# A recurrent segment loop with streamed weights: a step's small loads merged and laid out anew, and the output projection begun before the last group's values

## The chip, the cores and the metric

The kernel runs on one core of a Trainium2 chip. The metric is the device time of one execution in microseconds; the kernel before is given as the median of three runs.

## The reference, cut to what matters

Two independent parts share one launch. Part A is a long convolution over 2048 positions and 1024 channels; its result fills the first 1024 columns of the output. Part B is a recurrence over segments, and its result fills the other 1024:

```
kv = shift4(k, shift_k) * v
outA = q * (fftconv(kv, ssm_k) + kv * ssm_D)

mem = mem0                                  # 8 rows of 1024
for s in range(64):                         # segments of 32 rows of x
    h = concat([mem, x[32*s : 32*s+32]])    # 40 rows
    q, k, v = h @ Wq, h @ Wk, h @ Wv        # 32 heads of 128
    p = softmax(mask(q @ k^T / sqrt(128)))  # row i sees column j if i < 8 or j <= i
    o = (p @ v) @ Wo                        # 40 x 1024
    mem = o[:8]
    outB[32*s : 32*s+32] = o[8:]
```

Everything is bf16 at the borders. A step needs the eight output rows of the step before it, so the 64 steps can't overlap much; each reads all of Wq, Wk, Wv and Wo (8 MB each).

## The kernel before

The whole program is emitted in a manual schedule: each engine executes its instructions in the order in which the code issues them, and so does each DMA queue (SP's, ACT's and POOL's). Tiles of one tag share buffers, so a new tile waits until everything that reads or writes the old one has ended, its stores included.

**Prologue.** Part A is computed in stages by matmuls with Fourier matrices; its work runs up to about 0.3 ms. Interleaved with it, the class `Rows` (L126 to L193) does the work of Part B that doesn't depend on the recurrence: the projections of each segment's last eight rows of x (called memory-slot rows in the code), for all 64 segments at once. They are computed in twelve units, (q, g), (k, g) or (v, g), where g is one of four groups of eight heads. `half` runs half a block of matmuls, `evac` (L147) takes a block out of PSUM on ACT or DVE. When a k unit ends, the tile stq, which holds q and k of that group, is stored to QKBd in DRAM (L184, POOL's queue, 2 MB in runs of 16 KB); when a v unit ends, stv is stored to VBd (L187, POOL's queue, one DMA of 1 MB).

**Weights.** A pair is two weight blocks of [128, 1024] (512 KB). Most of the 64 pairs stay in SBUF, two are parked in PSUM and copied out by `unpark` (L715), and 17 are streamed in each step: STREAM (L40) lists which. `pairs` (L55) sets the order in which they are streamed. The ring has five buffers; `done` (L723) is called after a pair's last use, and `place` (L707) then issues the next pair's load on SP's queue, into the buffer that came free. So the loads stand in the order of use, and their order must be that of the steps.

**A step** (L906 to L967). hT holds the 32 rows of h: 8 of memory (from the step before) and 24 of x. For each group g: `qk_part` (L741) projects q and k with four column tiles of PE side by side into one PSUM bank, `qk_out` (L753) copies them to qks, `v_part` (L757) projects v into vacc and `v_out` (L770) copies it to vsb. `tr_a` (L780) transposes qks and writes QT and KT on DVE; KT also gets eight columns from qkb, the precomputed rows. `scores` (L801) makes S with the mask, `softmax` (L823) makes P and its transpose PT, `pv` (L836) multiplies by vsb and by VB (the precomputed values) in four PSUM tiles otacc, each evicted by ACT into OT; `wo` (L858) adds the group's contribution to Y. Within the loop, group g runs its own projections, scores and softmax of group g-1, and pv of group g-2. What is left for the tail (L943 on): wo of all groups, scores and softmax of group 3, pv of groups 2 and 3. At the end ACT copies Y to Y_sb, `fill_mem` (L885) transposes its first eight rows into the next hT, and the other 24 rows are stored by four DMAs on POOL's queue.

Small loads of a step:
- qkb, one per group, by `load_b` (L789) on SP's queue, issued in the group before: [128, 128] out of QKBd[g], 256 B per partition, 32 KB; two buffers.
- VB, by `load_vb` (L796), four DMAs of 16 KB on POOL's queue, issued in the tail ahead of group 3's wo.
- H, the 32 rows of x for the next step, by `load_h` (L652), one DMA of 64 KB on ACT's queue, issued at the start of group 2. It is read as "dq t c", a block of 32 rows for each quarter of the columns. H has the tag "st", as has Y_sb (L960): one buffer for both.
- OLd, a store of 64 KB on POOL's queue at the end of pv of group 3 (L856): it saves the attention output of the eight precomputed rows. Their output projection is done after the loop for all segments (L969 to L987).

Of the kernel before, what the change touches and what calls it, by code (L numbers as in the profile page):

```python
# [21 lines left out]
def fused_kernel(ctx: ExitStack, tc, q, k, v, shift_k, ssm_k, ssm_D, outa, x, mem0, Wq, Wk, Wv, Wo, outb, n_seg):  # L22
# [103 lines left out]
    class Rows:  # L126
# [27 lines left out]
        def half(self, n, by="A"):  # L154

            for _ in range(n):
# [21 lines left out]
                if lo:  # L178
                    if m == "v":
                        self.evac(self.sv[:, rb, cs], self.ps[:], by)  # L180
                    else:
                        self.evac(self.st[:, :, j, int(m == "k"), :], self.ps[:].rearrange("e (s r) -> e s r", r=8), by)
                    if m == "k" and j == 7:
                        nc.gpsimd.dma_start(QKBd[g].rearrange("e s x -> e (s x)"),  # L184
                                            self.st[:].rearrange("e s h t r -> e (s h t r)"))
                    if m == "v" and j == 7:
                        nc.gpsimd.dma_start(VBd.rearrange("(rb p) n -> p rb n", p=128)[:, :, g * 1024:(g + 1) * 1024],  # L187
                                            self.sv[:])
# [463 lines left out]
    def load_h(s):  # L652

        H_ = act.tile([128, 256], BF, tag="st", name="H")
        xq = x.rearrange("t (dq c) -> dq t c", dq=4)
        if s == 0:
            for dq in range(4):
                nc.gpsimd.dma_start(H_[32 * dq:32 * dq + 8, :], mem0[:, dq * 256:(dq + 1) * 256])
                nc.gpsimd.dma_start(H_[32 * dq + 8:32 * dq + 32, :], xq[dq, 0:24, :])
        else:  # L660
            nc.scalar.dma_start(H_[:], xq[:, 32 * s - 8:32 * s + 24, :])
        return H_

# [93 lines left out]
    def v_part(u, kcs):  # L757
        if kcs[0] == 0:
            u.vacc = ps_acc.tile([128, 512], F32, tag="acc", name="vacc")
        for kc in kcs:  # L760
            if kc % 2 == 0:
                w = pair(("v", u.g, kc // 2))
            for c in range(4):
                nc.tensor.matmul(u.vacc[32 * c:32 * c + 32, 0:256], lhsT=hT[:, kc, :],  # L764
                                 rhs=w[kc % 2][:, c * 256:(c + 1) * 256],
                                 start=(kc == 0), stop=(kc == 7), tile_position=(0, 32 * c))
            if kc % 2 == 1:
                done(("v", u.g, kc // 2))
# [11 lines left out]
    def tr_a(u):  # L780
# [4 lines left out]
        nc.vector.tensor_copy(u.KT[:, :, 32:40], u.qkb[:].rearrange("e (h t r) -> e t h r", h=8, t=2)[:, 1])  # L785
# [3 lines left out]
    def load_b(s, g):  # L789
        u = G()  # L790
        u.g = g
        u.qkb = act2.tile([128, 128], BF, tag="qkb", name="qkb")
        nc.sync.dma_start(u.qkb[:], QKBd[g][:, s, :])
        return u

    def load_vb(s):  # L796
        for c in range(4):
            nc.gpsimd.dma_start(VB[32 * c:32 * c + 32, :],  # L798
                                VBd[8 * s:8 * s + 8].rearrange("r (g c x) -> c g r x", g=4, c=4)[c])

    def scores(u):  # L801
        S = ps_ts.tile([128, 4, 40], F32, tag="ts", name="S")
        qb = u.qkb[:].rearrange("e (h t r) -> e h t r", h=8, t=2)
# [32 lines left out]
    def pv(u, s, cs, ts_bank=False):  # L836
# [3 lines left out]
        for c in cs:  # L840
            pool, tag = (ps_ts, "ts") if ts_bank and c == 2 else (ps_acc, "acc")
# [16 lines left out]
    def wo(u, Y, hhs=range(8)):  # L858
        for hh in hhs:
            if hh % 2 == 0:  # L860
                w = pair(("o", u.g, hh // 2))
            for dq in range(4):
                nc.tensor.matmul(Y[32 * dq:32 * dq + 32, 0:256], lhsT=u.OT[:, hh, 0:32],  # L863
                                 rhs=w[hh % 2][:, dq * 256:(dq + 1) * 256],
                                 start=(u.g == 0 and hh == 0), stop=(u.g == 3 and hh == 7),
                                 tile_position=(0, 32 * dq))
# [8 lines left out]
    def h_rows(H_, hT_, r0):  # L875
# [3 lines left out]
        for half in range(2):  # L879
# [3 lines left out]
            tp[:, 0:256].rearrange("p (hf dq r) -> p dq hf r", hf=2, dq=4)[:, :, :, r0:32])  # L883
# [15 lines left out]
    nxt = load_b(0, 0)  # L899
# [6 lines left out]
    for s in range(n_seg):  # L906
        us = []
        for g in range(4):
            if g == 2 and s + 1 < n_seg:
                H = load_h(s + 1)  # L910
# [5 lines left out]
            u = nxt  # L916
# [3 lines left out]
            if g < 3:  # L920
                nxt = load_b(s, g + 1)
            elif s + 1 < n_seg:
                nxt = load_b(s + 1, 0)
# [11 lines left out]
            v_part(u, range(0, 8))  # L935
            tr_a(u)
            v_out(u)
# [23 lines left out]
        nc.scalar.copy(Y_sb[:], Y[:, 0:256])  # L961
# [94 lines left out]
```

## Time and profile before

| | us |
|---|---|
| median of three runs | 2215.84 |
| lowest and highest run | 2213.84, 2217.09 |
| profiled execution, span on the core | 2198.5 |
| PE busy | 1808.6 (82%) |
| DVE busy | 1082.4 (49%) |
| ACT busy | 836.0 (38%) |
| POOL busy | 500.4 (23%) |

The profile's page gives the profiled execution's span, from its first instruction to its last, and no other time of that execution; the runs' times are taken from outside and are 17.3 us longer at the median. 732.29 MB moved by DMA in the span, 333 GB/s in the mean. How to read it: the share of an engine is over the whole span, which holds three different things, the prologue with Part A, the 64 steps, and the projection of the precomputed rows at the end; a window view cuts them apart. In the waits, "A <- B" means that A stood idle and B's end released it; the three numbers are the total in us, the number of times and the longest. In a timeline row stand the start, the duration, engine, line and operation, the output and the inputs, and in brackets the idle time before it with its releaser. The row of a DMA issue gives the time that the issuing queue took, not the transfer's.

### The profile page before, as it was taken

The page shows a single profiled execution, that of the slowest core. Times are in us where ns is not written, and L with a number is a line of the kernel's source. Part 1 is how long each engine was busy: PE and PEld are TensorE (multiplying, and loading weights), DVE is VectorE, ACT ScalarE, POOL GpSimd, SP SyncE. Part 2 cuts the span into 40 slices and gives each one's busy share as a digit, 9 for nine tenths or more (in the row PEclk, how much of TensorE's full clock was granted, in tenths as well). Part 3 has the DMA queues.
Part 4 walks back from the last instruction along what each step waited for, and adds up shares of the span by engine and source line. Part 5 has one row for each costly group of instructions (what it writes and reads, how often), then busy time and mean ns, then how long its engine had stood idle before and what let it go on. Part 6 is the DMA issues. An engine that isn't in the chain of part 4 may idle for free.

```text
span 2198.5 us, 88235 instructions
## 1 busy us (share of the span) xinstructions
PE 1808.6 (82%) x37779; PEld 1028.8 (47%) x37808; DVE 1082.4 (49%) x3235; ACT 836.0 (38%) x2538; POOL 500.4 (23%) x983
## 2 busy tenths in 40 slices
PE   4788877688888888788888878888888888888878
PEld 2332233354444445444544545544444445444558
DVE  6896822244544444444445445544444444444530
ACT  5456721133333334333333334333333333333320
POOL 4004622022222222222222222222222222222210
PEclk9999999899999999999999999999999999999999
DMA  7799889699999999999999999999999999999990
GB/s 255 267 353 350 302 302 369 248 354 345 343 341 365 344 358 367 339 342 333 349 352 361 365 357 364 364 345 353 358 353 347 349 347 361 323 348 345 357 328 21
DMA packets 275666, 732.29 MB, mean 333 GB/s; under 512 B 73323, under 2 KB 84539, under 8 KB 274761
## 3 DMA queue, kind: packets, MB, share of 16 engines
q1 hardware_dynamic: 242062, 683.06, 85.8%
q0 software_dynamic: 24320, 37.37, 5.2%
q10 hardware_dynamic: 8892, 6.23, 0.9%
q8 instruction: 295, 4.83, 0.9%
q14 instruction: 97, 0.79, 0.1%
HBM read 676.14 MB, written 59.18 MB: 334 GB/s over the span
## 4 chain that ended last, share of the span: by engine, by line
DMA 38%; PE 33%; issue 8%; DVE 3%; ACT 2%; POOL 1%; ACTq 1%; SPq 0%; POOLq 0%; DVEq 0%
PE qkacc L749 10%; DMA wring<-Wstv 10%; DMA wring<-Wstqk 8%; DMA wring<-Wsto 7%; PE yacc L863 6%; DMA out_dram<-Y_sb 5%; PE vacc L764 5%; DMA OLd<-OL 5%; PE otacc L846 3%; PE pl L979 3%; PE tp L777 2%; ACT OT L851 1%; PE otacc L848 1%; PE S L805 1%; DVE S L820 1%
## 5 line engine op out<-in xcount | busy, mean ns | idle before, releaser
L749 PE MATMUL qkacc<-Wqk,hT 128*32 128x512 bf16 x4096 | 354.6, 388 | 1.3 <-issue 1.3
L851 ACT CAST OT<-otacc 128x80 bf16<-128x80 f32 x1024 | 183.4, 233 | 438.6 <-PE otacc L848 391.2
L854 POOL COPY OL<-OT 128x64 bf16<-128x64 bf16 x252 | 63.3, 251 | 1221.9 <-ACT OT L851 1221.9
L764 PEld LDWEIGHTS <-hT 128*32 128x32 bf16 x8192 | 227.4, 98 | 190.1 <-issue 140.4
L749 PEld LDWEIGHTS <-hT 128*32 128x32 bf16 x8192 | 179.0, 98 | 215.4 <-issue 79.7
L863 PE MATMUL yacc<-Wo,OT 128*32 128x256 bf16 x5632 | 248.6, 278 | 22.2 <-issue 21.8
L863 PEld LDWEIGHTS <-OT 128*32 128x32 bf16 x8192 | 188.0, 97 | 103.5 <-issue 74.1
L764 PE MATMUL vacc<-Wv,hT 128*32 128x256 bf16 x5120 | 229.9, 279 | 2.7 <-issue 1.4
L749 PE MATMUL qkacc<-wring,hT 128*32 128x512 bf16 x2048 | 210.1, 398 | 24.3 <-DMA wring<-Wstqk 22.4
L764 PE MATMUL vacc<-wring,hT 128*32 128x256 bf16 x3072 | 145.4, 278 | 92.6 <-DMA wring<-Wstv 89.3
L846 PE MATMUL otacc<-PT,vsb 32*128 32x64 bf16 x2048 | 147.9, 192 | 55.3 <-ACT OT L851 49.1
L786 DVE COPY QT<-tp 128x256 bf16<-128x256 bf16 x256 | 74.7, 292 | 206.4 <-PE tp L777 198.8
L749 PE MATMUL qkacc<-Wearly,hT 128*32 128x512 bf16 x2048 | 171.0, 413 | 3.7 <-DVE hT L881 0.4
L718 ACT COPY wring<-park 128x1024 bf16<-128x1024 bf16 x128 | 129.9, 1015 | 110.4 <-PE qkacc L749 98.4
L755 ACT CAST qks<-qkacc 128x512 bf16<-128x512 f32 x256 | 150.5, 588 | 53.8 <-PE qkacc L749 48.6
L830 DVE TENSOR_REDUCE sm<-P 128x4 f32<-128x256 bf16 x256 | 107.6, 420 | 118.9 <-ACT P L828 118.9
L772 ACT CAST vsb<-vacc 128x256 bf16<-128x256 f32 x256 | 95.4, 373 | 179.2 <-PE vacc L764 178.2
L827 ACT ACTIVATE P<-S 128x128 bf16<-128x128 f32 x256 | 71.5, 279 | 238.3 <-DVE P L826 123.4
L819 DVE TENSOR_REDUCE mx<-S 128x4 f32<-128x160 f32 x256 | 83.2, 325 | 155.8 <-PE S L816 154.3
L863 PE MATMUL yacc<-wring,OT 128*32 128x256 bf16 x2520 | 131.5, 278 | 32.5 <-DMA wring<-Wsto 20.2
L798 POOL DMA_DIRECT2D VB<-VBd x256 | 152.3, 600 | 8.9 <-issue 3.6
L848 PE MATMUL otacc<-PT,VB 32*128 32x64 bf16 x2048 | 144.3, 188 | 8.9 <-issue 8.7
(218 smaller groups left out, 2830.0 us busy)
## 6 DMA issues: line engine op xcount, KB each, us to landing
wring<-Wstqk SPq DMA_DIRECT2D x448, 512.0 KB, 6.3
wring<-Wstv SPq DMA_DIRECT2D x320, 512.0 KB, 6.2
wring<-Wsto SPq DMA_DIRECT2D x315, 512.0 KB, 6.2
SK<-s_sb SPq DMA_DIRECT2D x8, 1024.0 KB
SU<-s_sb SPq DMA_DIRECT2D x8, 1024.0 KB, 5.4
QKBd<-stq POOLq DMA_DIRECT2D x4, 2048.0 KB, 9.8
Kg<-SK SPq DMA_DIRECT2D x16, 512.0 KB, 6.0
Ug<-SU SPq DMA_DIRECT2D x16, 512.0 KB, 8.0
```

What stands on the lines that cost most here:

```text
L718: nc.scalar.copy(t[:, 0, :], park[key][0][:])
L749: nc.tensor.matmul(u.qk[p0:p0 + 32, :], lhsT=hT[:, kc, :], rhs=w[t][:, c2 * 512:(c2 + 1) * 512], start=(kc == 0), stop=(kc == 7), tile_pos ...
L755: nc.scalar.copy(u.qks[:], u.qk[:])
L764: nc.tensor.matmul(u.vacc[32 * c:32 * c + 32, 0:256], lhsT=hT[:, kc, :], rhs=w[kc % 2][:, c * 256:(c + 1) * 256], start=(kc == 0), stop=(k ...
L772: nc.scalar.copy(u.v[:], u.vacc[:, 0:256])
L798: nc.gpsimd.dma_start(VB[32 * c:32 * c + 32, :], VBd[8 * s:8 * s + 8].rearrange("r (g c x) -> c g r x", g=4, c=4)[c])
L819: nc.vector.tensor_reduce(out=mx[:], in_=S[:], op=ALU.max, axis=AX.X)
L830: nc.vector.tensor_reduce(out=sm[:], in_=P[:], op=ALU.add, axis=AX.X)
L846: nc.tensor.matmul(o, lhsT=u.v[r, i * 128:(i + 1) * 128], rhs=PTv[r, i, 0], start=True, stop=False, tile_position=(32 * c, 0))
L848: nc.tensor.matmul(o, lhsT=VB[r, i * 128:(i + 1) * 128], rhs=PTv[r, i, 1], start=False, stop=True, tile_position=(32 * c, 0))
L851: nc.scalar.copy(u.OT[:, 2 * c:2 * c + 2, :], ov[:, :, 0:40])
L863: nc.tensor.matmul(Y[32 * dq:32 * dq + 32, 0:256], lhsT=u.OT[:, hh, 0:32], rhs=w[hh % 2][:, dq * 256:(dq + 1) * 256], start=(u.g == 0 and ...
```

## The change

1. QKBd is laid out by segment, then partition, then group; its store goes out on ACT's queue in runs of 256 B (8192 of them per store). VBd is laid out as the VB tile wants it; its store is 16 DMAs of 64 KB on POOL's queue for each v unit.
2. One qkb load for the whole step (128 KB, 1 KB per partition, one buffer), issued on SP's queue in the tail after group 3's scores. One VB load (64 KB), issued on POOL's queue at the very end of the step, behind the stores of the output. H is read in plain row order "(t dq) c", issued on ACT's queue in the tail after group 3's v_out, and has the tag "qks".
3. Group 3's v_part, tr_a and v_out leave the loop. The tail now begins with wo of group 0 (all eight heads), then tr_a, v_part and v_out of group 3, then scores, softmax and the rest. Y is a tile of the tag "acc" and uses columns 256 to 511 of its PSUM bank; group 3's v_part accumulates into columns 0 to 255 of the same bank, without a start flag of its own, because wo's start has cleared the bank. pv takes its PSUM tiles from the lists "aqaq" and "aqta" (a, q, t name the three pools). `h_rows` comes after the last wo. Y_sb has the tag "PT". The order of `pairs` follows: wo's group 0 ahead of v's group 3.

```diff
-    QKBd = dram.tile([4, 128, n_seg, 128], BF, name="QKBd")
+    QKBd = dram.tile([n_seg, 128, 4, 128], BF, name="QKBd")
-    VBd = dram.tile([n_seg * 8, 4096], BF, name="VBd")
+    VBd = dram.tile([n_seg, 4, 4, 8, 256], BF, name="VBd")
...
-    pairs += [("o", g, i) for g in range(4) for i in range(4)]
+    pairs[-4:-4] = [("o", 0, i) for i in range(4)]
+    pairs += [("o", g, i) for g in range(1, 4) for i in range(4)]
...
-                        nc.gpsimd.dma_start(QKBd[g].rearrange("e s x -> e (s x)"),
-                                            self.st[:].rearrange("e s h t r -> e (s h t r)"))
+                        nc.scalar.dma_start(QKBd[:, :, g, :].rearrange("s e x -> e s x"),
+                                            self.st[:].rearrange("e s h t r -> e s (h t r)"))
-                        nc.gpsimd.dma_start(VBd.rearrange("(rb p) n -> p rb n", p=128)[:, :, g * 1024:(g + 1) * 1024],
-                                            self.sv[:])
+                        for rb_ in range(4):
+                            for c in range(4):
+                                nc.gpsimd.dma_start(VBd[16 * rb_:16 * rb_ + 16, c, g],
+                                                    self.sv[:, rb_, c * 256:(c + 1) * 256])
...
-        H_ = act.tile([128, 256], BF, tag="st", name="H")
+        H_ = act.tile([128, 256], BF, tag="qks", name="H")
...
-            nc.scalar.dma_start(H_[:], xq[:, 32 * s - 8:32 * s + 24, :])
+            nc.scalar.dma_start(H_[:], x[32 * s - 8:32 * s + 24].rearrange("t (dq c) -> (t dq) c", dq=4))
...
-    def v_part(u, kcs):
+    def v_part(u, kcs, Y=None):
-            u.vacc = ps_acc.tile([128, 512], F32, tag="acc", name="vacc")
+            u.vacc = ps_acc.tile([128, 512], F32, tag="acc", name="vacc") if Y is None else Y
-                                 start=(kc == 0), stop=(kc == 7), tile_position=(0, 32 * c))
+                                 start=(kc == 0 and Y is None), stop=(kc == 7),
+                                 skip_group_check=Y is not None, tile_position=(0, 32 * c))
...
-        u.qkb = act2.tile([128, 128], BF, tag="qkb", name="qkb")
-        nc.sync.dma_start(u.qkb[:], QKBd[g][:, s, :])
+        qkb = act.tile([128, 4, 128], BF, tag="qkb", name="qkb")
+        nc.sync.dma_start(qkb[:], QKBd[s])
...
-        for c in range(4):
-            nc.gpsimd.dma_start(VB[32 * c:32 * c + 32, :],
-                                VBd[8 * s:8 * s + 8].rearrange("r (g c x) -> c g r x", g=4, c=4)[c])
+        nc.gpsimd.dma_start(VB[:], VBd[s].rearrange("c g r x -> (c g r) x"))
...
-    def pv(u, s, cs, ts_bank=False):
+    def pv(u, s, cs, banks="aaaa"):
-            pool, tag = (ps_ts, "ts") if ts_bank and c == 2 else (ps_acc, "acc")
+            pool, tag = {"a": (ps_acc, "acc"), "q": (ps_qk, "qk"), "t": (ps_ts, "ts")}[banks[c]]
...
-                nc.tensor.matmul(Y[32 * dq:32 * dq + 32, 0:256], lhsT=u.OT[:, hh, 0:32],
+                nc.tensor.matmul(Y[32 * dq:32 * dq + 32, 256:512], lhsT=u.OT[:, hh, 0:32],
-                                 start=(u.g == 0 and hh == 0), stop=(u.g == 3 and hh == 7),
-                                 tile_position=(0, 32 * dq))
+                                 start=(u.g == 0 and hh == 0), stop=(u.g in (0, 3) and hh == 7),
+                                 skip_group_check=u.g > 0, tile_position=(0, 32 * dq))
...
-            tp[:, 0:256].rearrange("p (hf dq r) -> p dq hf r", hf=2, dq=4)[:, :, :, r0:32])
+            tp[:, 0:256].rearrange("p (hf r dq) -> p dq hf r", hf=2, dq=4)[:, :, :, r0:32])
...
-            v_part(u, range(0, 8))
-            tr_a(u)
-            v_out(u)
+            if g < 3:
+                v_part(u, range(0, 8))
+                tr_a(u)
+                v_out(u)
...
-        Y = ps_qk.tile([128, 512], F32, tag="qk", name="yacc")
-        wo(us[0], Y, range(0, 4))
-        softmax(us[3], scores(us[3]))
-        wo(us[0], Y, range(4, 8))
-        pv(us[2], s, (0, 1))
+        Y = ps_acc.tile([128, 512], F32, tag="acc", name="yacc")
+        wo(us[0], Y)
+        tr_a(us[3])
+        v_part(us[3], range(0, 8), Y)
+        v_out(us[3])
+        if s + 1 < n_seg:
+            H = load_h(s + 1)
+        S = scores(us[3])
+        if s + 1 < n_seg:
+            qkb = load_b(s + 1)
+        softmax(us[3], S)
+        pv(us[2], s, (0, 1), "aqaq")
         wo(us[1], Y, range(0, 4))
-        pv(us[2], s, (2, 3))
+        pv(us[2], s, (2, 3), "aqaq")
         wo(us[1], Y, range(4, 8))
+        wo(us[2], Y)
+        pv(us[3], s, (0, 1, 2, 3), "aqta")
+        wo(us[3], Y)
         if s + 1 < n_seg:
             hT = new_hT()
             h_rows(H, hT, 8)
-        wo(us[2], Y)
-        pv(us[3], s, (0, 1))
-        pv(us[3], s, (2, 3), True)
-        if s + 1 < n_seg:
-            load_vb(s + 1)
-        wo(us[3], Y)
-        Y_sb = act.tile([128, 256], BF, tag="st", name="Y_sb")
-        nc.scalar.copy(Y_sb[:], Y[:, 0:256])
+        Y_sb = act.tile([128, 256], BF, tag="PT", name="Y_sb")
+        nc.scalar.copy(Y_sb[:], Y[:, 256:512])
...
             nc.gpsimd.dma_start(outb[32 * s:32 * s + 24, dq * 256:(dq + 1) * 256], Y_sb[32 * dq + 8:32 * dq + 32, :])
+        if s + 1 < n_seg:
+            load_vb(s + 1)
```

More of the change, by code (lines that the diff above doesn't have):

```diff
@@ L652, in load_h @@
     def load_h(s):
-        H_ = act.tile([128, 256], BF, tag="st", name="H")
-        xq = x.rearrange("t (dq c) -> dq t c", dq=4)
+        H_ = act.tile([128, 256], BF, tag="qks", name="H")
         if s == 0:
-            for dq in range(4):
-                nc.gpsimd.dma_start(H_[32 * dq:32 * dq + 8, :], mem0[:, dq * 256:(dq + 1) * 256])
-                nc.gpsimd.dma_start(H_[32 * dq + 8:32 * dq + 32, :], xq[dq, 0:24, :])
+            nc.gpsimd.dma_start(H_[0:32, :], mem0.rearrange("t (dq c) -> (t dq) c", dq=4))
+            nc.gpsimd.dma_start(H_[32:128, :], x[0:24].rearrange("t (dq c) -> (t dq) c", dq=4))
         else:
-            nc.scalar.dma_start(H_[:], xq[:, 32 * s - 8:32 * s + 24, :])
+            nc.scalar.dma_start(H_[:], x[32 * s - 8:32 * s + 24].rearrange("t (dq c) -> (t dq) c", dq=4))
         return H_
@@ L784, in tr_a, with load_b, new_u @@
         u.KT = act.tile([128, 8, 40], BF, tag="KT", name="KT")
[L785 removed]
+        nc.vector.tensor_copy(u.KT[:, :, 32:40], u.qkb.rearrange("e (h t r) -> e t h r", h=8, t=2)[:, 1])
         nc.vector.tensor_copy(u.QT[:].rearrange("e (c j) r -> e c j r", c=2), tv[:, 0])
         nc.vector.tensor_copy(u.KT[:, :, 0:32].rearrange("e (c j) r -> e c j r", c=2), tv[:, 1])
[L789 removed]
+    def load_b(s):
+        qkb = act.tile([128, 4, 128], BF, tag="qkb", name="qkb")
+        nc.sync.dma_start(qkb[:], QKBd[s])
+        return qkb
+    def new_u(g):
         u = G()
         u.g = g
[L792 to L793 removed]
+        u.qkb = qkb[:, g, :]
         return u
     def load_vb(s):
[L797 to L799 removed]
+        nc.gpsimd.dma_start(VB[:], VBd[s].rearrange("c g r x -> (c g r) x"))
     def scores(u):
         S = ps_ts.tile([128, 4, 40], F32, tag="ts", name="S")
[L803 removed]
+        qb = u.qkb.rearrange("e (h t r) -> e h t r", h=8, t=2)
         for c in range(4):
@@ L898, in fused_kernel @@
     load_vb(0)
-    nxt = load_b(0, 0)
+    qkb = load_b(0)
     for key in resident:
@@ L915, in fused_kernel @@
                     res[key] = res[at]
-            u = nxt
+            u = new_u(g)
             us.append(u)
```

6 lines of the change are left out of this document (removed).

## The prediction, made before the changed kernel was run

> **What bounds the kernel now.** I read the span first, then the window view cut into stages, then the DMA view, the waits and the timeline of the steps. A window row gives its stretch, us, busy of PE, PEld, DVE, ACT, POOL, granted TensorE clock, DMA share, GB/s.
>
> ```profile
> span 2198.5 us, 88235 instructions
> ...
> 0.00:404.80 404.80, 316.28 (x1565) 132.19 (x1598) 255.55 (x417) 189.54 (x293) 116.62 (x152) 0.94 0.85 304
> ...
> 448.90:2106.60 1657.70, 1391.47 (x34100) 814.42 (x34100) 798.39 (x2729) 622.55 (x2170) 372.10 (x807) 0.97 0.98 351
> ...
> L889 DVE COPY hT<-mt_tp x63: 191/192/193, 448.7 to 2106.4; 128x64 bf16<-128x64 bf16 x63
> ...
> q1 hardware_dynamic: 187511, 560.90, 93.0%
> ...
> q10 hardware_dynamic: 8184, 4.06, 0.9%
> ...
> wring<-Wstqk SPq DMA_DIRECT2D x434, 512.0 KB, 6.3
> ...
> qkb<-QKBd SPq DMA_DIRECT2D x248, 32.0 KB, 5.1
> VB<-VBd POOLq DMA_DIRECT2D x249, 16.0 KB, 5.3
> out_dram<-Y_sb POOLq DMA_DIRECT2D x248, 12.0 KB, 5.1
> H<-in_B_x_dram ACTq DMA_DIRECT2D x62, 64.0 KB
> ```
>
> The profiled execution has a span of 2198.5 us; the median of the runs is 2215.84, so 17.3 us lie around the span, and I leave those alone. The 63 fills of the memory rows (L889) mark the steps: the window from 448.9 to 2106.6 holds 62 of them in 1657.7 us, 26.74 us each. There the DMA engines are taken for 0.98 of the time and PE for 1391.47 of 1657.70, 84%. So a step is fed by DMA: the weights that don't fit are streamed.
>
> ```profile
> PE vacc L764 <- DMA wring<-Wstv: 62.7, 92, 2.4
> ...
> PE otacc L846 <- ACT OT L851: 48.2, 117, 2.3
> ...
> PE qkacc L749 <- DMA wring<-Wstqk: 22.4, 45, 1.7
> ...
> PE yacc L863 <- DMA wring<-Wsto: 20.2, 26, 2.4
> ...
> PE S L805 <- DVE KT L787: 14.4, 50, 0.5
> ...
> ACT OT L851 <- DMA out_dram<-Y_sb: 39.3, 12, 4.5
> ...
> 1245.00:1247.00 2.00, 1.86 (x68) 1.27 (x55) 1.37 (x5) 0.80 (x6) 0.00 (x0) 1.00 0.86 266
> 1275.00:1277.00 2.00, 1.41 (x45) 1.00 (x45) 0.59 (x2) 0.23 (x1) 0.03 (x1) 1.00 0.85 274
> ...
> 1265.00:1268.00 3.00, 2.38 (x63) 1.30 (x62) 1.25 (x6) 0.58 (x3) 0.00 (x0) 1.00 0.99 313
> ```
>
> PE stands for the ring 62.7 + 22.4 + 20.2 = 105.3 us in 62 steps, 1.70 a step; that bounds what any relief of the DMA engines can return. They aren't full everywhere: in the tail (two stretches of it are shown) the share drops to 0.86 and 0.85, 0.28 and 0.30 us free in each two microseconds. In the groups it is 0.99. Small loads cost time in the groups and are free in that much of the tail.
>
> **The step's loads.** One piece's time comes from the queues. On q10 (H alone) 0.9% of 16 x 1657.7 us are 238.7 us of engine time, or 3.85 per step for 128 pieces of 512 B: 30 ns a piece. q1 carries 17 pairs a step as 128 pieces of 4 KB, and 512 pieces of 256 B for qkb: 93.0% gives about 180 ns for 4 KB. The line through both gives 19 ns for 256 B and 51 ns for 1 KB. So today's qkb costs 512 x 19 / 16 = 0.62 us per step and the single one 128 x 51 / 16 = 0.41: 0.21 saved, bounded by 0 (if bytes alone count) and 0.55 (if 1 KB went like 256 B, rounded up). H costs 3.85 / 16 = 0.24. Both move from the fed groups into the tail: 0.86 us leave the groups, and 0.65 arrive in a tail with 0.30 free, so 0.35 come back. Net 0.51 us a step, between 0 and 1.70; in 63 steps **-32 us**.
>
> **The ACT stall.** H and Y_sb share the tag "st", so H's issue on ACT's queue waits for the output stores of Y_sb, with OT (L851) behind it: 39.3 us over 12 waits, and PE behind OT 48.2. H's new tag is that of qks, read out by then. Part of PE's share is the plain pace of pv; I take a third of 39.3, **-13 us**, between 0 and -48.
>
> **The order of the tail.** Its work for PE is the same; only the cover changes.
>
> ```profile
> 1199.64 0.39 PE L863 MATMUL yacc<-Wo,OT 128*32 128x256 bf16 x8
> ...
> 1200.08 0.39 PE L863 MATMUL yacc<-Wo,OT 128*32 128x256 bf16 x8
> ...
> 1200.53 0.37 ACT L961 CAST Y_sb<-yacc 128x256 bf16<-128x256 f32 x1 [0.78 <-PE yacc L863]
> ...
> 1206.05 0.32 DVE L819 TENSOR_REDUCE mx<-S 128x4 f32<-128x160 f32 x1 [0.29 <-PE S L816]
> ...
> 1208.43 0.45 DVE L834 STREAM_TRANSPOSE PT<-P 128x256 bf16<-128x256 bf16 x1
> ...
> 1210.64 0.21 PE L846 MATMUL otacc<-PT,vsb 32*128 32x64 bf16 x2
> ...
> L851 ACT CAST OT<-otacc 128x80 bf16<-128x80 f32 x1024 | 183.4, 233 | 438.6 <-PE otacc L848 391.2
> ```
>
> From mx to the end of PT softmax takes 2.83 us. Today wo 0 (second half), pv 2, wo 1, h_rows and wo 2 lie over group 3's; afterwards only pv 2, wo 1 and wo 2. Sixteen matmuls of wo in 0.44 us (from 1199.64 to 1200.08) make 0.88 for a group, and pv 2 with four evictions of 0.233 from two banks takes 0.6 to 0.93: 2.4 to 2.7 of cover, 0.15 to 0.45 us bare a step. Against that, PE's wait for KT (14.4 us, 0.23 a step) gets v_part between tr_a and scores, and h_rows fills the time in which PE waits for Y_sb. I cost the order at **0**, from +0.45 to -0.4 a step.
>
> New waits. PT takes Y_sb's buffer, so the first softmax of a step waits on DVE for the output stores. Y_sb is done at 1200.90 and four issues of 0.57 (L856's median, below) follow, so the last starts at 1202.6 and lands 5.1 later, at 1207.7; PT is written at 1208.43 and read at 1210.64. So 0.7 us hide it on DVE and 2.9 on PE; with that gone KT and QT, queued behind PT on DVE, hold PE's scores by the excess. VB is issued after them on POOL, at 1203.2, and lands 5.3 later at 1208.5, before pv reads it at 1210.64: free, the excess bare if later than that. qkb waits on SP for scores with ring loads behind it, at a time when the ring is full: free, and at most the 0.30 above if not. SP and POOL issue three loads fewer each, off PE's path. v_part in Y's bank and wo's other half change no instruction's length; h_rows' copy reads at another stride, from 0 to another 192 ns (L889's own), beside ACT's 0.37 of Y_sb.
>
> **The prologue.** The stores are now written in small pieces, once.
>
> ```profile
> 360.92 0.54 POOL L184 DMA_DIRECT2D QKBd<-stq  x1
> ...
> 371.77 0.59 ACT L149 CAST stq<-ps_q 128x512 bf16<-128x512 f32 x1 [12.23 <-DMA QKBd<-stq]
> ...
> 404.45 0.56 POOL L184 DMA_DIRECT2D QKBd<-stq  x1 [22.68 <-issue]
> ...
> 413.07 1.28 SPq L112 DMA_DIRECT2D Wo<-in_B_Wo_dram  x3
> ...
> 429.69 0.62 PE L764 MATMUL vacc<-wring,hT 128*32 128x256 bf16 x8 [19.58 <-DMA wring<-Wstv]
> ...
> 236.32 0.80 POOL L187 DMA_DIRECT2D VBd<-stv  x1 [0.38 <-ACT stv L149]
> ...
> 238.19 1.17 POOL L572 TENSOR_TENSOR Yre<-pa,pb 128x512 bf16<-128x512 bf16 x1
> ...
> 291.35 1.07 ACT L149 CAST stv<-ps_v 128x512 bf16<-128x512 f32 x2 [5.04 <-DMA VBd<-stv]
> ...
> 303.81 0.59 PE L641 MATMUL y_ps<-zt,G2h 128*128 128x512 bf16 x1 [4.80 <-DMA zt<-SZ]
> ...
> QKBd<-stq POOLq DMA_DIRECT2D x4, 2048.0 KB, 9.8
> ...
> L856 POOL DMA_DIRECT2D OLd<-OL x62 | 35.3, 569 | 21.2 <-POOL OL L854 18.1 <-issue 3.1
> ...
> L941 SPq DMA_DIRECT2D Wearly<-OLd x2: 751/5534/10316, 2120.9 to 2122.2; - x2
> ```
>
> A QKBd store becomes 8192 pieces of 256 B: 9.9 us at 19 ns over 16 engines and about 2 of latency, 19.8 + 2 if a written piece costs twice a read one (my outer bound, no row has such a write); now 9.8 to landing. Third store: stq's next writer already waits 12.23 us for it, so its excess counts almost in full, +5 (3 to 14). Fourth: the Wo loads at 413.07 take the memory it is read from, the ring's loads are queued about them, and the first step waits 19.58 us, +5 (3 to 13). The issue of the first two now stands in ACT's queue, where evictions follow; the trace has no store of 8192 pieces, but of the two loads of 4096 (L941) the first took 0.75 us to issue and the second 10.3 behind it: +3 (0 to 16). A VBd store becomes 16 issues on POOL at 569 ns, 9.1 us in place of 0.80. At 236.32 Yre stands behind it with the convolution's product: +7 (4 to 14). At 285 ACT already waits 5.04 and PE then 4.80 for zt: +2.5 (0 to 5). The last one delays output stores: +2 (0 to 2). In sum **+25 us**, 10 to 64.
>
> The Trainium skill, "DMA: Bandwidth & Descriptors", Specifications, speaks against this part: pieces under 512 B are read, modified and written. No row here shows such a store. By that rule the two late stores take the upper ends above, 27 in place of 10, and the prologue +42.
>
> **Sum:** -32 - 13 + 25 = -20, on the profiled execution 2198.5 - 20 = 2178.5, with the 17.3 around it **2196 us**. A measurement of this kernel can tell some 0.2% (4.4 us) from no change.
>
> **Rivals.**
> (1) The prologue costs more than the steps give: third and fourth store 14 + 13, issue on ACT 10, VBd 14 + 5 + 2, in sum 58 against 45 gained: 2229. It decides once the prologue's loss passes 45. For it: ACT's and PE's waits already end on these stores. Against: half of that price is doubled write time, which nothing here shows.
> (2) The DMA engines are bound by bytes whatever the place: the tail's free share is only the ring's refill running out, so H and qkb cost there what they did. Then only 0.21 x 63 = 13 come back, the ACT stall was hidden, the prologue stays: 2216 - 13 + 25 = 2228. For it: 0.98 over the whole window.
> (3) The engines are loaded unevenly and H evens out. q10 shows 8184 packets in 62 loads, 132 each: 128 pieces and 4 more, where the 1054 ring loads and 248 of qkb on q1 have 62 x (17 x 128 + 512) = 166656 pieces in 187511 packets, 16 more each. So H, cut as 4 blocks, seems to lie on four engines: 32 x 30 ns = 0.96 us there instead of 0.24. The others stand idle behind them, and read in order "(t dq)" it spreads. The most that full engines could return is the 2.5% (41 us) missing in the queues' sum of 97.5%, and 13 for the pieces: 2216 - 54 + 25 = 2187. Against: 1265 to 1268, behind an H load, is at 0.99.
> The Trainium skill, same page, "Why a DMA increments its semaphore by 16 and not by 1", says that a transfer takes the largest k up to 16 that divides its slowest dimensions, so 4 for H before and 16 after; the 132 packets agree, and by it the sum would be case 3's 2187.
> (4) The bare softmax costs 0.30 us a step, the middle of 0.15 to 0.45, and nothing offsets it: 19 us; 2216 - 45 + 25 + 19 = 2215, no change.
>
> **Chances.** Forecast (2185 to 2211 by itself) 0.37; case 3 (2165 to 2190) 0.20; case 1 0.17; case 2 0.14; case 4 0.12. The likeliest gives 2196. The range runs from 2160 (54 gained in the engines, 12 of ACT's stall, prologue at its low 10) to 2240 (13 gained, prologue 37). Faster: 0.37 + 0.20 = 0.57. Same: case 4, 0.12. Slower: cases 1 and 2, 0.31.
>
> **What would show it.** In the steps' window: PE's waits for the ring below 105 us; no wait of OT for out_dram; a step near 26.0 us; q1 with 432 packets fewer a step (three loads' 48 and 384 pieces); H with 144 packets, not 132. Before it: the first step's fill later than 448.7 by about 25, ACT's wait for stq above 12.23, Yre behind sixteen VBd issues. Wrong if the step keeps its 26.74 us, if otacc waits for PT in the tail for more than 0.45 a step, if PT waits for out_dram, or if the fill marks move by more than 45.

## The result, and the profile after

| | before | after |
|---|---|---|
| median of 16 runs, us | 2212.2 | 2189.27 |
| lowest to highest | 2188.93 to 2224.86 | 2175.66 to 2198.84 |
| profiled span | 2198.5 | 2187.2 |
| first step's fill | 448.7 | 490.4 |
| step, mean of 62 | 26.74 | 25.88 |
| last fill to the end of the span | 92.1 | 92.1 |

The ratio of the runs is 0.9922, 95% interval 0.9901 to 0.9942: 0.8% faster, some 17 us (13 to 22). The forecast of 20 us less and 2196 us held in sign and size. It is the difference of two larger things, which the spans show: 62 steps give back 62 x 0.855 = 53.0 us, and the first fill (the copy of the first new memory rows into hT, which marks the start of the repeated steps) comes 41.7 us later; 11.3 us remain between these two spans. The medians are 22.9 apart; single executions of one kernel spread by more than 20 us, and the ratio leaves out runs in a slower state.

The windows of the kernel after (us, busy PE, PEld, DVE, ACT, POOL, granted clock, DMA share, GB/s) and the fills that cut them:

```profile
0.00:404.80 404.80, 294.82 (x1412) 118.96 (x1413) 247.00 (x404) 184.67 (x285) 137.93 (x195) 0.91 0.85 288
...
490.60:2095.10 1604.50, 1354.83 (x34101) 829.74 (x34100) 806.49 (x2728) 622.18 (x2170) 254.75 (x618) 0.98 0.98 362
...
L893 DVE COPY hT<-mt_tp x63: 180/191/192, 490.4 to 2095.1; 128x64 bf16<-128x64 bf16 x63
```

In the steps the DMA share is 0.98 as before, but it carries 362 GB/s instead of 351: the same bytes in less time, not engines with more leisure. In the first 404.8 us it is the other way, 0.85 both times and 288 instead of 304. The queues of the steps (packets, MB and share of 16 engines), and H's load, whose last number is its landing, the time from the issue to the arrival of the data:

```profile
q1 hardware_dynamic: 160641, 560.58, 93.7%
q0 software_dynamic: 11904, 11.21, 2.3%
q8 instruction: 267, 4.37, 1.1%
q10 hardware_dynamic: 8928, 4.07, 0.9%
q14 instruction: 79, 0.65, 0.1%
...
H<-in_B_x_dram ACTq DMA_DIRECT2D x62, 64.0 KB, 6.0
```

q1 has 26870 packets fewer, 433 a step (432 were worked out). H's load has 8928 / 62 = 144 packets instead of 132, and now a landing time stands in its row. What PE and DVE waited for in the steps:

```profile
PE vacc L765 <- DMA wring<-Wstv: 59.7, 98, 2.3
...
PE otacc L850 <- ACT OT L855: 48.0, 110, 1.2
...
PE qkacc L750 <- DMA wring<-Wstqk: 19.0, 36, 1.4
...
PE x_tp L884 <- DMA H<-in_B_x_dram: 10.3, 22, 1.6
...
PE mt_tp L892 <- ACT Y_sb L964: 5.7, 24, 0.3
...
DVE PT L838 <- DMA out_dram<-Y_sb: 2.9, 2, 1.6
...
PE yacc L867 <- DMA wring<-Wsto: 0.6, 3, 0.2
```

PE's waits for the ring fell from 105.3 to 59.7 + 19.0 + 0.6 and 0.5 in v_part's Y, 79.8 us; the wait for Y_sb from 29.5 to 5.7, at the price of 10.3 for H. ACT's wait for the output stores is gone from the list, PT's for the same stores is 2.9 us, covered as worked out. But PE's wait for OT is 48.0 us, as it was.

The prologue of the kernel after: the third QKBd store and stq's next writer, and the DMA view of the stretch of the fourth store, which runs alone; below it the same store before.

```profile
393.11 0.38 ACTq L185 DMA_DIRECT2D QKBd<-stq  x1
...
409.44 0.59 ACT L150 CAST stq<-ps_q 128x512 bf16<-128x512 f32 x1 [16.36 <-DMA QKBd<-stq]
```

```profile
q10 hardware_dynamic: 8208, 2.10, 88.4%
...
QKBd<-stq ACTq DMA_DIRECT2D x1, 2048.0 KB, 11.2
```

```profile
q0 software_dynamic: 272, 2.16, 65.2%
...
QKBd<-stq POOLq DMA_DIRECT2D x1, 2048.0 KB, 8.5
```

The stretches are 11.5 and 8.6 us long: 8208 packets take 0.884 x 11.5 = 10.2 us of all sixteen engines, 19.8 ns each, where the long runs (with the first VB loads) took 0.652 x 8.6 = 5.6. The landings, 11.2 against 8.5, differ by less than that.

### The profile page after: what moved, and what is told of

It reads as the page before. It is cut to its first block, busy times and chain, and to the rows that moved or that the text cites. A ratio compares the mean times of both kernels' runs of the same rounds, so it can differ in the third digit from the quotient of the medians.

```text
span 2187.2 us, 87959 instructions
## 1 busy us (share of the span) xinstructions
PE 1783.4 (82%) x37808; PEld 1048.2 (48%) x37808; DVE 1090.5 (50%) x3235; ACT 835.3 (38%) x2538; POOL 405.9 (19%) x841
## 4 chain that ended last, share of the span: by engine, by line
PE 47%; DMA 36%; issue 6%; DVE 4%; ACT 4%; POOL 1%; SPq 0%; ACTq 0%; DVEq 0%; POOLq 0%
DMA wring<-Wstv 17%; PE qkacc L750 13%; PE yacc L867 9%; DMA wring<-Wstqk 7%; PE vacc L765 4%; PE otacc L850 3%; PE yacc L765 3%; PE tp L779 3%; PE pl L984 3%; DMA QKBd<-stq 2%; DMA H<-in_B_x_dram 2%; PE ps_k L177 2%; PE otacc L852 1%; DMA wring<-Wsto 1%; PE ps_q L177 1%
## 5 line engine op out<-in xcount | busy, mean ns | idle before, releaser
L765 PEld LDWEIGHTS <-hT 128*32 128x32 bf16 x8192 | 213.8, 97 | 168.7 <-issue 101.9
L750 PEld LDWEIGHTS <-hT 128*32 128x32 bf16 x8192 | 178.3, 96 | 209.9 <-issue 66.7
L867 PE MATMUL yacc<-Wo,OT 128*32 128x256 bf16 x5632 | 253.3, 282 | 26.6 <-issue 21.2
L867 PEld LDWEIGHTS <-OT 128*32 128x32 bf16 x8192 | 213.1, 99 | 90.4 <-issue 58.4
L765 PE MATMUL vacc<-wring,hT 128*32 128x256 bf16 x2560 | 118.0, 277 | 74.7 <-DMA wring<-Wstv 73.5
L823 DVE TENSOR_REDUCE mx<-S 128x4 f32<-128x160 f32 x256 | 83.1, 325 | 163.8 <-PE S L820 160.7
L765 PE MATMUL vacc<-Wv,hT 128*32 128x256 bf16 x3584 | 158.4, 274 | 0.7 <-issue 0.7
L852 PE MATMUL otacc<-PT,VB 32*128 32x64 bf16 x2048 | 144.2, 189 | 11.2 <-issue 10.5
L867 PE MATMUL yacc<-wring,OT 128*32 128x256 bf16 x2520 | 137.1, 281 | 16.4 <-issue 15.4
L885 DVE COPY hT<-x_tp 128x192 bf16<-128x192 bf16 (+1 forms) x64 | 23.0, 359 | 233.8 <-PE x_tp L884 233.8
L970 POOL DMA_DIRECT2D out_dram<-Y_sb x256 | 129.1, 511 | 39.6 <-ACT Y_sb L964 36.3
L850 PEld LDWEIGHTS <-vsb 32*128 32x128 bf16 x2048 | 84.3, 92 | 103.8 <-issue 94.1
```

What stands on the lines that cost most here:

```text
L750: nc.tensor.matmul(u.qk[p0:p0 + 32, :], lhsT=hT[:, kc, :], rhs=w[t][:, c2 * 512:(c2 + 1) * 512], start=(kc == 0), stop=(kc == 7), tile_pos ...
L823: nc.vector.tensor_reduce(out=mx[:], in_=S[:], op=ALU.max, axis=AX.X)
L850: nc.tensor.matmul(o, lhsT=u.v[r, i * 128:(i + 1) * 128], rhs=PTv[r, i, 0], start=True, stop=False, tile_position=(32 * c, 0))
L852: nc.tensor.matmul(o, lhsT=VB[r, i * 128:(i + 1) * 128], rhs=PTv[r, i, 1], start=False, stop=True, tile_position=(32 * c, 0))
L867: nc.tensor.matmul(Y[32 * dq:32 * dq + 32, 256:512], lhsT=u.OT[:, hh, 0:32], rhs=w[hh % 2][:, dq * 256:(dq + 1) * 256], start=(u.g == 0 an ...
```

## The experiments

**The theory after the result:** the small-piece stores cost the whole delay of the prologue, through engine time and through the buffers that wait for them; the steps' gain comes from the loads of H and qkb (moved, merged, spread) and from the freed issue of H on ACT's queue, not from the tail's order. **Rivals:** part of the delay is step 0's own; the order gives half of the gain; H's four engines (case 3) give much of it. All ratios are to the kernel before, run beside on the same chip, but not all rows come from one chip. Fill and step are those of the one profiled execution. Its step can be off by some 0.3 us (e5 below shows it; the profiled executions of e5 and e9 were the fastest of their kernels), and its fill by some 4: in the eight kernels with both stores as before it lies between 446.4 and 453.9.

| kernel | ratio, 95% interval | first fill | step |
|---|---|---|---|
| after | 0.9922 (0.9901 to 0.9942) | 490.4 | 25.88 |
| e1 both stores alone | 1.0146 (1.0095 to 1.0196) | 487.3 | 26.74 |
| e2 QKBd store alone | 1.0102 (1.0049 to 1.0155) | 473.4 | 27.01 |
| e3 VBd store alone | 1.0064 (1.0031 to 1.0096) | 464.1 | 26.90 |
| e10 after, QKBd store on POOL | 0.9925 (0.9891 to 0.9959) | 494.9 | 25.88 |
| e6 Y_sb's tag alone | 1.0181 (1.0142 to 1.0219) | 451.6 | 27.43 |
| e8 tag, VB behind the stores | 0.9935 (0.9904 to 0.9966) | 446.4 | 26.47 |
| e7 order and tags | 1.0139 (1.0103 to 1.0175) | 451.7 | 27.38 |
| e9 order, tags, VB behind | 0.9918 (0.9889 to 0.9948) | 446.6 | 26.23 |
| e5 H in row order alone | 0.9957 (0.9923 to 0.9991) | 447.6 | 26.26 |
| e11 after, H in four blocks | 1.0374 (1.0326 to 1.0422) | 492.0 | 27.50 |
| e4 after, stores of before | 0.9794 (0.9756 to 0.9832) | 453.9 | 26.12 |
| e12 e4, H sooner | 0.9825 (0.9775 to 0.9875) | 453.1 | 26.05 |

**Both stores alone (e1).** The kernel before with the change's lines for the two layouts and the two stores; the step's loads keep number and place and read the new layouts:

```diff
...
-        nc.sync.dma_start(u.qkb[:], QKBd[g][:, s, :])
+        nc.sync.dma_start(u.qkb[:], QKBd[s][:, g, :])
...
-                                VBd[8 * s:8 * s + 8].rearrange("r (g c x) -> c g r x", g=4, c=4)[c])
+                                VBd[s][c].rearrange("g r x -> (g r) x"))
```

> The kernel before with only the two stores of the prologue and their layouts changed; a step's loads stay four of qkb and four of VB, at their old places. Theory (the small-piece stores cost the whole delay of the prologue): the first step's fill, 448.7 us before and 490.4 after the full change, comes at 485 to 492; the steps stay at 26.7 us; the time is +42 us, ratio about 1.019. Rival (part of the delay is step 0's own, from the new order of the streamed pairs and the moved loads): fill at 455 to 478, ratio 1.004 to 1.013.

The fill came 38.6 us late and the step stayed at 26.74: the stores alone make 38.6 of the 41.7. The 3 that are left for step 0 are within the spread of the fills. In the runs' ratio it is 1.5%, 32 us (21 to 43).

**Each store alone (e2, e3).** The same edit for QKBd only, and for VBd only.

> The kernel before with only QKBd's layout and store changed (256 B pieces, ACT's queue; the step's loads read the new layout with the same pieces). Both stores together gave a first fill at 487.3 us instead of 448.7 and ratio 1.0146. Theory (a store now takes the 16 engines 9.8 us instead of 5.0, and each of the four delays the loads behind it): this half gives 18 to 26 of the 38.6 us, fill at 467 to 475, ratio 1.007 to 1.011. Rival (the VBd issues on POOL are the larger part, as the prediction's terms had it per unit): fill at 453 to 462, ratio 1.001 to 1.006.

> The kernel before with only VBd's layout and store changed (16 DMAs on POOL's queue for each v unit). Theory: the second half of the prologue's delay, 12 to 20 us (stv held 10 us and Yre 9 us in the second stage), fill at 461 to 469, ratio 1.004 to 1.009. Rival (VBd nearly all, or nearly nothing): fill at 475 or more, or at 455 or less.

The fills move by 24.7 and 15.4 us, in sum 40.1: the parts add up, and QKBd is the larger. Where QKBd's 24.7 arise, its own stores tell. The second and third store of e2 with the line that has the first, and the same of before (its third stands in the prediction, at 360.92):

```profile
L184 ACTq DMA_DIRECT2D QKBd<-stq x4: 366/372/437, 116.0 to 426.8; - x4
...
199.09 0.38 ACTq L184 DMA_DIRECT2D QKBd<-stq  x1
...
379.38 0.37 ACTq L184 DMA_DIRECT2D QKBd<-stq  x1
```

```profile
L184 POOL DMA_DIRECT2D QKBd<-stq x4: 540/560/568, 113.2 to 404.5; - x4
...
187.18 0.56 POOL L184 DMA_DIRECT2D QKBd<-stq  x1
```

At the first store e2 is 2.8 us behind already, before a small piece is written; the executions on record, alike up to there, start it between 110.8 and 116.0. By the second store it is 11.9 us behind, by the third 18.5, and only 6.2 come after it. So 9.1 us arise between the first two stores and 6.6 between the second and the third. The 9.1 aren't chance: 73.5 to 76.4 us lie between the first two stores in the nine kernels whose QKBd store is that of before, 83.1 to 84.8 in the four that write it in small pieces from ACT's queue. The issue itself takes 0.38 us, so ACT isn't held. The windows behind the first store, of e2 and then of before, show what is:

```profile
120.00:125.00 5.00, 5.00 (x16) 1.90 (x15) 4.72 (x8) 1.46 (x3) 0.00 (x0) 0.66 1.21 320
...
130.00:135.00 5.00, 4.02 (x20) 1.72 (x19) 4.72 (x8) 2.80 (x5) 0.00 (x0) 1.00 0.65 190
...
140.00:150.00 10.00, 1.45 (x3) 0.21 (x2) 9.29 (x14) 0.00 (x0) 0.00 (x0) 0.55 1.02 393
```

```profile
120.00:125.00 5.00, 5.00 (x20) 2.11 (x19) 4.71 (x8) 2.05 (x4) 0.00 (x0) 0.81 0.98 402
140.00:150.00 10.00, 9.78 (x42) 4.23 (x42) 9.47 (x15) 5.92 (x8) 0.00 (x0) 0.88 1.00 372
```

While the store runs, the full engines carry 320 GB/s instead of 402 (the fewer matmuls of that window go with its lower clock, 0.66 against 0.81). But from 130 to 135 they are free for a third of the time, and in the 10 us from 140 PE does 3 matmuls instead of 42. The end of that pause, in e2's timeline:

```profile
150.55 0.61 PE L176 MATMUL ps_q<-hTB,Wqk 128*128 128x512 bf16 x1 [5.29 <-DMA Wqk<-in_B_Wq_dram]
```

It is a weight load of the next unit that comes late. Why, SP's queue shows: its wait for the store, and its first issue behind that wait, in e2; then the same issue in before.

```profile
SPq L112 <- DMA QKBd<-stq: 8.6, 1, 8.6
...
133.50 0.33 SPq L112 DMA_DIRECT2D Wqk<-in_B_Wq_dram  x1
```

```profile
121.25 0.70 SPq L112 DMA_DIRECT2D Wqk<-in_B_Wq_dram  x1
```

For 8.6 us SP issues nothing, until the first store has landed, 17.4 us after its issue; counted from the store, the unit's loads go out 9.4 us later than before, and that is the size of the 9.1. The loads don't need the store: before issues the same one at 121.25, and its own store, which took 11.5 us, landed only at 124.7. The second and third store of e2 hold SP in the same way, for 10.1 and 12.7 us, and those of after, e1 and e11 for 9.4 to 13.3; where POOL issues the store (before, e3, e10), SP has no such wait at these three places. So a load behind the store is late because it is issued late, and not only because the engines are taken. Why SP waits for a store of ACT's queue isn't shown.

VBd works otherwise. The waits from 187 to 380 us, of before and then of e3:

```profile
PE ps_v L173 <- ACT stv L149: 2.7, 1, 2.7
...
PE z_ps L582 <- POOL Yre L572: 0.9, 1, 0.9
```

```profile
PE ps_v L173 <- ACT stv L149: 10.5, 1, 10.5
PE z_ps L584 <- POOL Yre L574: 8.7, 2, 7.9
```

7.8 us more for the buffer stv and 7.8 for Yre behind the sixteen issues: with 15.6 in sum, these two are e3's 15.4.

**The QKBd store on POOL's queue (e10).** The kernel after with the first store's queue changed.

```diff
-                        nc.scalar.dma_start(QKBd[:, :, g, :].rearrange("s e x -> e s x"),
+                        nc.gpsimd.dma_start(QKBd[:, :, g, :].rearrange("s e x -> e s x"),
```

> The kernel after the change with QKBd's store issued on POOL's queue instead of ACT's, pieces and layout unchanged. Theory (the pieces' engine time counts, 9.8 us a store; ACT's issues took only 0.4 us each): first fill at 485 to 500, ratio as the kernel after's, 0.988 to 0.998. Rival (the queue on ACT delays evictions): fill at 480 or less, ratio 0.985 or less. If POOL's issue of 8192 pieces is slow it shows there as a long DMA instruction, and the fill comes later than 500.

```profile
L185 POOL DMA_DIRECT2D QKBd<-stq x4: 2778/2790/2803, 115.4 to 442.0; - x4
```

The ratio is the same, the fill 4.5 us later, which is within its spread, and the issue takes 2.8 us on POOL. So the choice of the queue doesn't change the total, and the pieces are what the kernels with the late fill share. But it does change the way: SP's three waits for the store are gone, and instead POOL's own queue stands 6.5 us for the first store's landing (17.5 us) with VBd's stores behind it, and PE 8.4 us for stv, where it stood 3.3 in the kernel after. That both ways cost the same was not foreseen; a small-piece store on a queue for which nothing waits wasn't tried.

**Y_sb's tag alone (e6), and with VB behind the output stores (e8).**

```diff
-        Y_sb = act.tile([128, 256], BF, tag="st", name="Y_sb")
+        Y_sb = act.tile([128, 256], BF, tag="PT", name="Y_sb")
...
-        if s + 1 < n_seg:
-            load_vb(s + 1)
         wo(us[3], Y)
...
             nc.gpsimd.dma_start(outb[32 * s:32 * s + 24, dq * 256:(dq + 1) * 256], Y_sb[32 * dq + 8:32 * dq + 32, :])
+        if s + 1 < n_seg:
+            load_vb(s + 1)
```

e6 is the first pair of lines, e8 all of it.

> The kernel before with only Y_sb's tag changed from st to PT, so that H's load no longer waits for the output stores. Forecast's term: ACT's 39.3 us of waiting vanish and a third of it reaches the time, -13 us, ratio 0.994. Rival A (PE's wait for OT is pv's own pace and was 48.2 before and 48.0 after the change): nothing, ratio 0.998 to 1.002. Rival B (the whole wait was on the path): -39 us, ratio 0.982.

> The kernel before with Y_sb's tag PT and the four VB loads issued behind the output stores. Y_sb's tag alone made the step 27.43 us, PT standing 110.2 us for the output stores. Theory (the stores were late because POOL issues the VB loads ahead of them, 4 x 0.6 us): PT's wait falls below 15 us and the step to 26.5 to 26.7, since the H load's stall is gone too; ratio 0.993 to 0.999. Rival (sharing PT's buffer is itself too tight without the new order of the tail): PT waits 50 us or more, step 27.0 to 27.4, ratio above 1.006.

All three expectations of e6 missed: it is 1.8% slower. The waits of e6, then of e8:

```profile
PE S L805 <- DVE KT L787: 114.3, 109, 5.2
DVE PT L834 <- DMA out_dram<-Y_sb: 110.2, 55, 5.9
...
PE otacc L846 <- ACT OT L851: 30.6, 108, 0.6
```

```profile
PE otacc L846 <- ACT OT L851: 28.4, 97, 0.6
...
PE S L805 <- DVE KT L787: 14.0, 44, 1.5
...
DVE PT L834 <- DMA out_dram<-Y_sb: 4.1, 3, 2.1
```

H is free in e6 (OT's share of PE's waits falls from 48.2 to 30.6), but PT stands for the output stores, and KT behind it holds PE's scores for 114.3 us. The prediction had 0.7 us of cover with the stores first; four VB issues of 0.6 us ahead of them take 2.4, so 1.7 a step would be bare, and 110.2 / 62 = 1.78 is. With VB behind, the wait is 4.1 us in all and the kernel 0.65% faster than before.

**The tail's order with the tags (e7), and with VB behind (e9).** The kernel after's tail; stores, layouts, and H's and qkb's loads as before. e9 differs from e7 by VB's place alone:

```diff
-        if s + 1 < n_seg:
-            load_vb(s + 1)
         wo(us[3], Y)
...
+        if s + 1 < n_seg:
+            load_vb(s + 1)
```

> The kernel before with the tail's new order (output projection first, group 3's values in its bank, h_rows after the last projection, tags of Y_sb and H apart), stores, layouts, and the count and place of the loads as before. Theory (the order gives about half of the step's 0.86 us: PE's wait for Y_sb 29.5 to about 7 and for the ring's wo pairs 20.2 to about 1): step at 26.2 to 26.4 us, ratio 0.986 to 0.991. Rival (the forecast's: order is neutral and the relief of the DMA engines in the groups gives it all): step at 26.6 to 26.8, ratio 0.997 to 1.003.

> The tail's new order, the tags apart, and the VB loads behind the output stores; stores, layouts and the other loads as before (so the order run of 27.38 us a step with POOL's order mended). Theory: PT's wait below 15 us, step 26.2 to 26.4, ratio 0.985 to 0.992; the order is worth some 0.3 us beyond the tag. Rival (the relief of the DMA engines in the groups, by moved and merged loads, gives the step's gain): step 26.6 or more, ratio 0.997 or above.

e7 fails as e6 does. e9 has the step and the ratio that its theory named, but e8 comes nearly as far without the order. e9 against e8 is the order by itself: 0.9918 against 0.9935, 0.17 points with an uncertainty of 0.43 (9 us). PE's wait for Y_sb does fall (29.1 to 16.2 us), and that for OT rises from 28.4 to 51.3:

```profile
PE otacc L848 <- ACT OT L853: 51.3, 117, 1.4
...
PE mt_tp L890 <- ACT Y_sb L964: 16.2, 59, 1.2
```

So the order alone isn't told from nothing. The 48.0 us of the kernel after, above, are thus two things: H's stall went out of that row (e8), and the new order put a wait of its own in (e9). Why pv waits longer there wasn't tried.

**H's row order, alone in before (e5) and undone in after (e11).**

```diff
-            nc.scalar.dma_start(H_[:], xq[:, 32 * s - 8:32 * s + 24, :])
+            nc.scalar.dma_start(H_[:], x[32 * s - 8:32 * s + 24].rearrange("t (dq c) -> (t dq) c", dq=4))
```

h_rows and the first step's loads go with it; e11 is the reverse edit in the kernel after.

> The kernel before with H read in plain row order (and h_rows reading it so), nothing else. Case 3 of the prediction (H on four engines holds the others up): H has 144 packets a load, the ring waits fall, step 26.74 to 26.1 to 26.4, ratio 0.988 to 0.994. Theory (the share was 0.98 to 0.99 behind H loads, so unevenness costs little): step 26.6 to 26.8, ratio 0.997 to 1.002.

> The kernel after the change with H read in four blocks as before, issued in the tail; nothing else. Case 3: ring waits and the step grow, 25.88 to 26.2 to 26.5, ratio against before 0.998 to 1.005, and H lands later than its present 6.0 us, so x_tp's wait of 10.3 grows. Theory: only H's own landing matters, at most 0.3 us a step: 25.9 to 26.2, ratio 0.991 to 0.999.

Alone, the order brings 0.4% (0.1 to 0.8): some 9 us, 0.15 a step, between the two expectations; the profiled step of 26.26 says 0.48 and is too quick, for that execution was the fastest of its twelve. In the kernel after, the reverse costs 4.5%, beyond both. Its waits, its queue, and three of the H loads in its chain of waits (start, us, what):

```profile
PE x_tp L886 <- DMA H<-in_B_x_dram: 106.7, 47, 6.2
```

```profile
q10 hardware_dynamic: 8184, 4.06, 0.9%
```

```profile
1195.40 7.16 DMA H<-in_B_x_dram
1222.38 8.12 DMA H<-in_B_x_dram
1249.76 10.27 DMA H<-in_B_x_dram
```

Again 132 packets: if the load lies on four engines, each has 32 pieces to pass through a full queue instead of 8. Of the loads that stand in the chain the longest takes 11.6 us, where the longest in the kernel after's chain takes 7.2. Issued in group 2, as before the change, that was hidden; issued in the tail, PE waits.

**The version with the stores of before (e4), and H sooner (e12).** The kernel after with QKBd, VBd and their stores as before.

```diff
-        nc.sync.dma_start(qkb[:], QKBd[s])
+        nc.sync.dma_start(qkb[:], QKBd[:, :, s, :].rearrange("g e x -> e g x"))
-        nc.gpsimd.dma_start(VB[:], VBd[s].rearrange("c g r x -> (c g r) x"))
+        for c in range(4):
+            nc.gpsimd.dma_start(VB[32 * c:32 * c + 32, :],
+                                VBd[8 * s:8 * s + 8].rearrange("r (g c x) -> c g r x", g=4, c=4)[c])
```

In e12 H's load stands between group 3's tr_a and its v_part instead of behind v_out; the rest is e4.

> The kernel after the change with the stores and layouts of before; the step's loads are merged as far as that allows (one qkb load of 512 pieces of 256 B, four VB loads). Theory: the first fill goes back to 449 to 455, the steps keep nearly all, 25.88 + 0.21 = 26.1 us; time about 2212 - 53 + 13 = 2172, ratio 0.982, and 0.99 against the kernel after. Rival (the step's gain hangs on the new layout's long pieces): steps at 26.5 or more, ratio 0.992 or above.

> The version with the stores of before and the step of after (2165.68 us, ratio 0.9794), with H's load issued ahead of group 3's v_part instead of behind its v_out. There PE's x_tp waited 21.4 us for H. Theory: that wait falls below 5 us and the step from 26.12 to 25.8 us, ratio 0.971 to 0.977. Rival (the ring's loads behind H are late by as much, or ACT waits for the transposes): step 26.0 to 26.2, ratio 0.977 to 0.983.

e4 beats both kernels: 2165.68 us, 0.9794, fill at 453.9, step 26.12. The new layout's long pieces are worth the 0.24 us a step that it lacks in the profile, in 62 steps 15 us, as far as two single executions can tell; the stores for them cost 36.5 us of the fill, more than twice that. In e12 the wait for H goes and the time doesn't move. The waits of e4, then of e12:

```profile
PE x_tp L884 <- DMA H<-in_B_x_dram: 21.4, 31, 2.9
...
PE qkacc L748 <- DMA wring<-Wstqk: 14.6, 24, 1.6
```

```profile
PE qkacc L748 <- DMA wring<-Wstqk: 24.8, 41, 1.8
```

Of H's 21.4 us, 10.2 came back as waits for the ring. The two ratios can't be told apart.

## Why the prediction was right, point by point

**The DMA relief, -32 us: right in sum, not in its parts.** From e9 to e4 (H and qkb moved into the tail, H spread and with its own tag) the ratio falls by 1.24 points, 27 us with some 10 of uncertainty; the two profiles show only 7 of it, for e9's execution was 12 us under its median. The long pieces of qkb come on top, 0.24 us a step in the profile where 0.21 was worked out. The prediction priced H at 0.24 us of evenly spread time; e5 shows that its block order cost about 0.15 more. Case 3 was therefore part of what happened: its 54 us for the steps are nearer to the 53.0 measured than the forecast's 45. The Trainium skill, "DMA: Bandwidth & Descriptors", "Why a DMA increments its semaphore by 16 and not by 1", gives four engines for the old pattern and sixteen for the new by its rule; 132 and 144 packets agree in four kernels.

The forecast had the engines save 0.21 us a step by longer pieces, and let 0.30 come out of the tail's free time and 0.21 out of ACT's stall. The queues' shares say otherwise. They sum to 97.5% before and to 98.1% after, so of a step the engines were taken for 26.07 us before and for 25.39 after, and free for 0.67 and 0.49. Of the 0.86 us, 0.68 are work that got shorter and only 0.18 free time that was filled. In e4, whose pieces are still short, the engines were taken for 25.75, so about half of the 0.68 isn't the length of the pieces. The steps of before, e1, e2 and e3, which should be alike, lie between 25.97 and 26.23, so this half is larger than their scatter; why the same pieces took less time wasn't tried.

**The ACT stall, -13 us: right in size, on a condition.** e8 gives 0.65%, 14 us (7 to 21). The condition is POOL's order. The prediction reckoned its 0.7 us of cover with the output stores going out first, as the change has them, but gave that place no price of its own: without it the same tag costs 40 us.

**The order of the tail, 0: not contradicted.** Between e8 and e9 lie 0.17 points with an uncertainty of 0.43, which leaves room for 0.2 us a step either way. The bare softmax of case 4 didn't show in the time, and no wait of PE's otacc for PT stands among those of the kernel after.

**The prologue, +25 us: the term that was too small**, by 14 to 17 us in the profiles (38.6 to 41.7); the runs' ratio of e1, 32 us (21 to 43), doesn't exclude 25. VBd was put at 7 + 2.5 + 2 and measured 15.4: Yre's 7 was 7.8, but stv's 2.5 was 7.8. The larger miss is the QKBd term, 5 + 5 + 3 against 24.7, of which 2.8 stand ahead of the first store. The two late stores were dearer in the prediction than in the run (10 against 6.2). The two early ones were put at 3, for the issue on ACT's queue, and cost 15.6 with what they trail: ACT's queue was the wrong place to look, its issue takes 0.38 us, while SP's queue stood 8.6 and 10.1 us until they had landed. The prediction set 9.9 + 2 us for the new store against 9.8 for the old, each by itself; beside the other traffic the first new store landed after 17.4 us and the old one after 11.5. The duration of a piece, 19 ns, was right (19.8).

The Trainium skill, same page, Specifications, would have had these pieces read, modified and written, and gave +42 in the prediction. The sum came close to it, but not that way: 19.8 ns a written piece leaves no room for a doubling against the 19 of a read one, and its late stores would have had to cost 27, where they cost 6.2.

**Rivals.** Case 1 (prologue above 45) came within 4 us of deciding in the profiles, but not by its parts: its two late stores, at 27, cost 6.2. Case 2, by which only 13 us come back, is refuted by e4, which gets 45 back (37 to 54) with the old stores. Two errors, 8 us of gain and 14 to 17 of loss, partly cancel; that the time was met so closely is luck in that part.

## What to carry to other kernels

Price a store by what stands until it has landed, on every queue, and not only by what it adds on the queue that issues it: here 8192 small pieces added some 5 us of engine time and 6 us of landing beside other traffic (17.4 against 11.5), and another queue's loads went out 9 us late for it. A buffer shared with an outgoing store is as good as the store's place in its queue: look at what is issued ahead of it. Before a load is moved closer to its use, count its packets: here one with the packets of four engines instead of sixteen landed late, and only the old distance hid that.

## What was not expected of the hardware

The profiled run of the kernel after took 2189.17 us with a span of 2187.2, so 2.0 us lie around a span; the 17.3 of the prediction were mostly the spread of runs (2188.93 to 2224.86 for the kernel before). The prediction added and subtracted them alike, so its time wasn't touched. A queue's issue of 8192 pieces took 0.38 us on ACT and 2.79 on POOL. With the issue on ACT, SP's queue stood for the store's landing, 8.6 to 13.3 us at each of the first three stores of four kernels.
